# Moving sums of x, output transposes and ScalarE's bank fills in a fused attention and MLP kernel

## The chip, the cores and the metric

The kernel runs on one core of a Trainium2 chip. A core has five engines that take their instructions in order, each from its own queue, and wait for each other by semaphores: TensorE (PE in the profile; its weight loads are PEld), VectorE (DVE), ScalarE (ACT), GpSimd (POOL) and SyncE (SP), which here only issues DMAs. Times are device microseconds of one execution; the kernel before took 877.88 us in the median of three runs (873.69 to 878.38).

## The reference

Attention with a hash mask over 4 batches of 8 heads, 768 positions and 64 numbers a head, then an MLP over its 3072 tokens of 512:

```python
q_bits = (np.einsum('bhsd,dk->bhsk', q, proj) > 0).astype(np.int64)
k_bits = (np.einsum('bhsd,dk->bhsk', k, proj) > 0).astype(np.int64)
...
mask = q_bucket[:, :, :, None] == k_bucket[:, :, None, :]
scores = np.where(mask, scale * np.matmul(q, k.transpose(0, 1, 3, 2)), -1000000000.0)
attn = softmax(scores)            # with 1e-09 added to the sum
x = np.matmul(attn, v)            # brought to (3072, 512)
h = x @ w_in                      # 512 -> 2048
g = np.maximum(h, 0.0) + alpha * np.minimum(h, 0.0)
return (g @ w_out).astype(np.float32)
```

## The kernel before

`fast_path` first does the attention, in 16 pairs of heads, up to about 313 us. It stores x in DRAM (`x_s`), and rounds and stores the weights (`w_in_s`, `w_out_r`, `w_out_s`). Then comes the MLP, one batch of 768 tokens after the other, and this is where the change lies.

Both products of the MLP are done in the manner of Strassen and Winograd: a product of 2 by 2 blocks takes seven block products, on sums and differences of the blocks. The sums are made by VectorE, the products by TensorE in PSUM, and the results are put together in PSUM or by ScalarE and VectorE. `Product` (L899) is one such product in steps named 1, 2, 22, 5, 6, 3, 7, 4: each a few matmuls into one of three banks a, b, c, and a copy or a sum that reads the bank. A step's matmuls add to what stands in the bank, so ScalarE first fills ("seeds") a bank where the next sum is to start from an earlier result.

A batch b goes through 8 blocks of kind "1" (`ff1`, L966: x by w_in, with `g` made from it), n = 0 to 7, and 7 blocks of kind "2" (`ff2`, L1229: g by w_out, itself one of seven products, in the order 1, 2, 5, 6, 3, 7, 4), n = 0 to 6. The rows name the products `f_0` to `f_7` and `z_1` to `z_7`, with the bank's letter after it (`z_4a`).

For batches 1 to 3 four of the blocks "1" share two products that are done once, one level deeper: `unit(b, u, before)` (L1134), u = 0 ahead of block 0 and u = 1 ahead of block 4. A unit holds two `Inner` products, `one` and `two`, whose banks are named `na` to `nf`, and works in between the last step of the block before (`before.step(4)`) and the first steps of the block that follows. Its results are tiles named `n`. The blocks "1" after it are of the class `Rest` (L994): their step 1 seeds banks a and b with the one result, their step 5 seeds c with the other.

What each part needs from VectorE:

- `sum_x(b, n, DVE)` (L886): one subtraction of 128 by 768, making one of the four sums of x of the batch: n = 0 makes x3 from x5 and x0, n = 1 a new x5, n = 2 x4, n = 3 x6.
- `sum_inner_x(b, o)` (L1054): three subtractions (L1062 to L1064) for the nested level, `xn`; o = 0 reads x0, o = 1 reads x3.
- `sum_inner(b, u, o)` (L1046): four sums of the weights of the nested level (L1051), in batch 1 only, which are also stored by GpSimd for the later batches.
- `sum_w2(b, n, ...)` and `sum_g2(b, n, ...)` (L1211, L1221): the sums `ws` and `gs` for the next block "2". The first `sum_w2` of a block waits for the load `wl` of its part of w_out (`load_w2`, L1182).
- `turn_out()` (L1269): for each finished part of the output, two transposes by VectorE and 12 DMAs to the output, on SyncE's queue. The parts become ready at the last step of the blocks 2, 3, 7 and 4 (the entries are `m2`, `m3`, `m5`, `m4`), the last of them, `m4`, inside the unit of the next batch.

The order of the work on TensorE, VectorE, ScalarE and for most of GpSimd is the program's: `do` keeps an instruction behind all that was traced before it on its engine. DMAs are placed by the scheduler, as soon as it takes their inputs and buffers to be ready, unless they are `pinned`, which puts them behind the DMA that was traced just before on the same queue. The output DMAs of batches 0 to 2 and the loads of `load_inner` (L1021) are pinned; `load_w` (L893), which loads the `wi` weights of a block "1" three blocks ahead into one of three buffers, is not, from its fourth call on.

The loop over the blocks is at L1472. In iteration n of kind "2" it computes block n while the sums of block n + 1 are made; at its end it makes the next product and does `before.step(4)`. In blocks 6 of batches 0 to 2 it makes `sum_inner_x(b + 1, 0)`, `sum_x(b + 1, 0)`, later `sum_inner_x(b + 1, 1)`; the other three `sum_x` stand in the unit. `turn_out()` is called at the end of every iteration but the last.

Of the kernel before, what the change touches and what calls it, by code (L numbers as in the profile page):

```python
# [407 lines left out]
def fast_path(  # L408
# [14 lines left out]
    B, H, S, D = q.shape  # L423
# [20 lines left out]
    PE, DVE, ACT, POOL = nc.tensor, nc.vector, nc.scalar, nc.gpsimd  # L444
# [253 lines left out]
    def two_banks(name):  # L698
        return psum.tile([P, 2, 512], F32, name=name, tag="sc", bufs=3)
# [172 lines left out]
    def pinned(when, ins):  # L872

        if when:
            do(ins)
# [10 lines left out]
    def sum_x(b, n, engine):  # L886

        to, a, c = ((3, 5, 0), (5, 2, 5), (4, 2, 3), (6, 4, 1))[n]
        if to != 5:
            x_m[b, to] = mid.tile([P, 2, CW], F32, name=f"x{b}_{to}", tag=f"x{to}", bufs=1)  # L890
        do(engine.tensor_tensor(x_m[b, to], x_m[b, a], x_m[b, c], op=ALU.subtract))
# [102 lines left out]
    class Rest(Product):  # L994
# [5 lines left out]

        def step(self, n):
            if n == 1:
                self.seed("a", self.p1)
                self.seed("b", self.p1)
            elif n == 5:
                self.seed("c", self.p5)
            elif n == 6:
                self.times("a", 4, 4, False)
                self.keep("a", "u1")
            elif n == 7:  # L1010
                self.times("a", 5, 5, False)
                self.keep("a", "u2")
                self.finish("22", self.p5, self.sb["u2"])
            else:
                super().step(n)
# [38 lines left out]
    def sum_inner_x(b, o):  # L1054

        x = x_m[b, 3 * o]
        if o == 0:
            t = mid.tile([P, 4, HC], F32, name=f"xn{b}_0", tag="x", bufs=1)
        else:
            t = late[0].tile([P, 4, HC], F32, name=f"xn{b}_1", tag="gs5", bufs=1)  # L1060
        left, right = (x[:, :, c * HC : (c + 1) * HC] for c in range(2))
        do(DVE.tensor_tensor(t[:, :2], right, x[:, 0].rearrange("p (c w) -> p c w", c=2), op=ALU.subtract))  # L1062
        do(DVE.tensor_tensor(t[:, 2], right[:, 1], t[:, 0], op=ALU.subtract))
        do(DVE.tensor_tensor(t[:, 3], left[:, 1], t[:, 2], op=ALU.subtract))  # L1064
        n_x[b, o] = {0: left[:, 0], 1: left[:, 1], 2: right[:, 1], 3: t[:, 0], 4: t[:, 2], 5: t[:, 1], 6: t[:, 3]}
# [68 lines left out]
    def unit(b, u, before):  # L1134

        def bank(name, tag=None):
            name = f"n{name}{b}_{u}"
            return psum_bc[0].tile([P, 512], F32, name=name, tag=tag) if tag else two_banks(name)[:, 0]

        one = Inner(b, u, 0, bank("a"), bank("b", "b"), bank("c"))  # L1140
        one.step(1)
        one.step(5)
        before.step(4)
        one.step(2)
        one.step(6)
        if u:
            sum_w2(b, 0, 3, 4)
        else:
            sum_inner(b, 0, 1)
            for n in range(1, 4):  # L1150
                sum_x(b, n, DVE)
        two = Inner(b, u, 1, bank("d"), bank("e", "b"), bank("f", "c"))
        two.step(1)
        one.step(3)
        two.step(5)
        one.step(7)
        two.step(2)
        two.step(6)
        one.step(4)
        two.step(3)  # L1160
        now = ff1(b, 4 * u)
        now.step(1)
        two.step(7)
        now.step(2)
        now.step(5)
        two.step(4)
        if u:
            sum_w2(b, 0, 6, 5)
        return now

    def new_g(b, m):
# [39 lines left out]
    def sum_w2(b, n, *ms):  # L1211

        if n < 7:
            for m in ms:
                x, op, y = {
                    3: (21, ALU.add, 2), 4: (3, ALU.subtract, 0), 5: (0, ALU.subtract, 21), 6: (1, ALU.subtract, 4),
                }[m]
                w2[b, n, m] = t = late[0].tile([P, HK, H2], F32, name=f"ws{b}_{n}_{m}", tag=f"ws{m}", bufs=1 + (m < 5))
                do(DVE.tensor_tensor(t, w2[b, n, x], w2[b, n, y], op=op))  # L1219
# [49 lines left out]
    def turn_out():  # L1269
        while to_turn:  # L1270
            b, p, half, ch = to_turn.pop(0)
            o = late[0].tile([P, CW, 2], F32, name=f"o{b}_{p}", tag="o")
            for i in range(2):
                do(DVE.transpose(o[:, :, i], m2[b, p][:, i]))  # L1274

            src = o.rearrange("p (c w d) i -> p c w (d i)", c=CH, d=32)
            for a in range(DM // 128):
                for c in range(CH):
                    cols = slice(half * DM // 2 + 64 * a, half * DM // 2 + 64 * a + 64)
                    queue = nc.gpsimd if (b, p) == (B - 1, 3) and c % 2 else nc.sync  # L1280
                    pinned(b + 1 < B, queue.dma_start(  # L1281
                        out_v[b, ch * CH + c].rearrange("(w r) d -> r w d", r=32)[:, :, cols],
                        src[32 * a : 32 * a + 32, c],
                    ))
# [184 lines left out]
    blocks = [(b, what, n) for b in range(B) for what, count in (("1", NI), ("2", 7)) for n in range(count)]  # L1469


    for j, (b, what, n) in enumerate(blocks):  # L1472
        n2 = n + 1 if what == "2" else 0 if n == NI - 1 else 7
        if n2 == 0:
            sides_g(b, 0)
            if b == 0:
                sum_w2(b, 0, 3, 4)
        if not j:
            now.step(6)
        elif not (b and what == "1"):  # L1480
            now.step(2)
        if j == 0:
            now.step(3)
            now.step(7)
            now.step(2)
        now.step(22)
        if (b, what, n) == (1, "2", 1):
            largest()
        if what == "2" and n == 6 and b + 1 < B:
            sum_inner_x(b + 1, 0)  # L1490
            sum_x(b + 1, 0, DVE)
        if b and what == "1" and n == 1:
            load_inner(b, 1)
        if b and what == "1" and n in (2, 3):
            sum_inner(b, 1, n - 2)
        if 0 < n2 < 7:
            sides_g(b, n2)
            sum_w2(b, n2, 3, 4)
        if n2 < 7:
            sum_g2(b, n2, 3, 4)  # L1500
        if j:
            if not (b and what == "1"):
                now.step(5)
            now.step(6)
            now.step(3)
            if n2 or b == 0:
                sum_w2(b, n2, 6)
            if what == "2" and n == 6 and b + 1 < B:
                sum_inner(b + 1, 0, 0)
            if b and what == "1" and (n + 1) % 4:  # L1510
                after = ff1(b, n + 1)
                after.step(1)
            now.step(7)
            if n2 or b == 0:
                sum_w2(b, n2, 5)
            sum_g2(b, n2, 5)
        if (b, what, n) == (1, "2", 3):
            verdict()

        for n_out in [(), (0,), (1,), (2, 3), (4,), (5, 6), (7,)][j] if j < 7 else ():  # L1520
            sum_out(n_out)
        for n_out in [(1,), (2, 3), (4,), (5, 6), (7,)][j] if j < 5 else ():
            load_out(n_out)
        if what == "1":
            load_w(b * NI + n + 3)

            if b and n in (2, 5):
                load_w2(b, n // 4)
            if not b and n >= NI - 2:
                load_w2(b, n - NI + 2)  # L1530
        else:
            load_w2(b, n + 2)
            if b + 1 < B:
                if n == 5:
                    load_inner(b + 1, 0)
                if n == 0:
                    load_x(b + 1)
                if n == 6:
                    sum_inner_x(b + 1, 1)
        if j + 1 < len(blocks):  # L1540
            turn_out()
        else:
            turn_last(0)
        before = now
        if j + 1 < len(blocks):
            b1, what1, n1 = blocks[j + 1]
            if b1 and what1 == "1" and n1 % 4 == 0:
                now = unit(b1, n1 // 4, before)
            elif b1 and what1 == "1":
                now = after  # L1550
                now.step(2)
                now.step(5)
                before.step(4)
            else:
                now = ff1(b1, n1) if what1 == "1" else ff2(b1, n1)
                now.step(1)
                before.step(4)
        else:
            before.step(4)
        if n2 < 7:  # L1560
            sum_g2(b, n2, 6)
# [29 lines left out]
```

## Time and profile before

| | |
|---|---|
| median of three runs | 877.88 us (873.69 to 878.38) |
| the profiled execution | 873.89 us, span 872.1 us |
| TensorE busy | 855.7 us, 98% of the span |
| VectorE busy | 752.3 us, 86% |
| ScalarE busy | 415.7 us, 48% |
| GpSimd busy | 123.6 us, 14% |
| granted TensorE clock, mean | 0.997 |
| units of batches 1, 2, 3 with u = 0 start at about | 449, 589, 726 us |

The page gives the busy time of each engine; a timeline gives the instructions in order of time as "start, duration, engine, line, operation, output <- inputs, shapes, count", and in brackets how long the engine had been idle before it and who ended that. Idle time of an engine that isn't the bound costs nothing by itself. A table by stretches gives each engine's busy time in a stretch, the clock that TensorE was granted, and what the DMA engines moved. The end of a matmul is modelled, so the pauses between matmuls tell more than their durations.

### The profile page before, as it was taken

The page shows a single profiled execution, that of the slowest core. Times are in us where ns is not written, and L with a number is a line of the kernel's source. Part 1 is how long each engine was busy: PE and PEld are TensorE (multiplying, and loading weights), DVE is VectorE, ACT ScalarE, POOL GpSimd, SP SyncE. Part 2 cuts the span into 40 slices and gives each one's busy share as a digit, 9 for nine tenths or more (in the row PEclk, how much of TensorE's full clock was granted, in tenths as well). Part 3 has the DMA queues.
Part 4 walks back from the last instruction along what each step waited for, and adds up shares of the span by engine and source line. Part 5 has one row for each costly group of instructions (what it writes and reads, how often), then busy time and mean ns, then how long its engine had stood idle before and what let it go on. Part 6 is the DMA issues. An engine that isn't in the chain of part 4 may idle for free.

```text
span 872.1 us, 15105 instructions
## 1 busy us (share of the span) xinstructions
PE 855.7 (98%) x5602; PEld 591.8 (68%) x5602; DVE 752.3 (86%) x1210; ACT 415.7 (48%) x778; POOL 123.6 (14%) x265
## 2 busy tenths in 40 slices
PE   9999999999999999999989999999999999999996
PEld 4444444444444445569986759997668998577996
DVE  6999999999999977899896969896769897768986
ACT  6777888877788823321115441114452113453111
POOL 1322423332433210210000100000000000000001
PEclk9999999999999999999999999999999999999999
DMA  8855879889697536775343934342845334650242
GB/s 198 187 135 130 207 180 232 176 198 235 132 270 188 169 134 226 251 275 192 126 132 99 331 114 165 122 166 58 314 142 177 141 109 132 211 203 9 97 155 68
DMA packets 180035, 147.97 MB, mean 170 GB/s; under 512 B 126976, under 2 KB 161968, under 8 KB 176368
## 3 DMA queue, kind: packets, MB, share of 16 engines
q1 hardware_dynamic: 166688, 118.92, 46.7%
q0 software_dynamic: 10256, 26.66, 10.0%
q10 hardware_dynamic: 3008, 1.33, 0.6%
q8 instruction: 46, 0.75, 0.4%
q14 instruction: 37, 0.30, 0.1%
HBM read 115.35 MB, written 30.41 MB: 167 GB/s over the span
## 4 chain that ended last, share of the span: by engine, by line


## 5 line engine op out<-in xcount | busy, mean ns | idle before, releaser
L790 ACT ACTIVATE pt<-sc 128x768 f32<-128x768 f32 x192 | 153.9, 812 | 3.0 <-PE sc L787 2.8
L787 PE MATMUL sc<-qT,kT 64*128 64x384 f32 x768 | 155.2, 482 | 0.0
L820 PE MATMUL av<-pt,vn 128*32 128x385 f32 (+1 forms) x1536 | 127.0, 485 | 0.0
L820 PEld LDWEIGHTS av<-pt,vn 128*32 128x32 f32 x1536 | 50.4, 109 | 73.8 <-issue 68.6
L787 PEld LDWEIGHTS sc<-qT,kT 64*128 64x128 f32 x768 | 68.2, 187 | 38.1 <-issue 38.0
L983 DVE TENSOR_TENSOR g<-g,g 128x384 f32<-128x384 f32 (+1 forms) x92 | 63.5, 711 | 1.6
L787 PE MATMUL sc<-qb,kb 64*128 64x384 bf16 x384 | 63.3, 323 | 0.8 <-DVE alpha L563 0.4
L979 DVE SCALAR_TENSOR_TENSOR g<-h,alpha 128x384 f32<-128x384 f32 x63 | 37.9, 614 | 26.8 <-ACT h L972 26.8
L1281 POOL DMA_DIRECT2D out_dram<-o x4 | 2.2, 560 | 367.0 <-DVE o L1274 367.0
L1227 DVE TENSOR_TENSOR gs<-g,gs 128x768 f32<-128x768 f32 x56 | 53.3, 952 | 1.0
L1227 DVE TENSOR_TENSOR gs<-g 128x768 f32<-128x768 f32 x56 | 53.2, 951 | 0.0
L1219 DVE TENSOR_TENSOR ws<-wl 128x512 f32<-128x512 f32 x56 | 38.5, 687 | 15.9 <-DMA wl<-w_out_s 15.0
L787 PEld LDWEIGHTS <-kb 64*128 64x128 bf16 x384 | 19.4, 94 | 34.9 <-issue 11.7
L607 ACT ACTIVATE wr<-raw 128x512 int32<-128x512 uint32 x32 | 22.1, 690 | 30.7 <-DVE wsi L651 15.4
L798 DVE TENSOR_TENSOR accp<-pt,pt 128x1536 f32<-128x1536 f32 x16 | 28.1, 1756 | 7.2 <-ACT pt L790 7.2
L748 POOL DMA_DIRECT2D qb<-hr x60 | 30.0, 506 | 26.4 <-ACT hr L743 26.4
L803 DVE TENSOR_TENSOR accd<-accd,pt 128x1536 f32<-128x1536 f32 x16 | 28.1, 1758 | 1.7
L809 DVE TENSOR_TENSOR accd<-accd,accp 128x1536 f32<-128x1536 f32 x16 | 28.1, 1758 | 0.6
L806 DVE TENSOR_TENSOR accp<-accp,pt 128x1536 f32<-128x1536 f32 x16 | 28.0, 1753 | 0.0
L802 DVE TENSOR_TENSOR accd<-pt,pt 128x1536 f32<-128x1536 f32 x16 | 28.0, 1751 | 0.0
L1431 ACT ACTIVATE qT<-qT 128x768 f32<-128x768 f32 x15 | 12.7, 845 | 25.0 <-DMA kb<-hr 20.6
L1239 DVE TENSOR_TENSOR m<-m,m 128x768 f32<-128x768 f32 x24 | 22.7, 946 | 0.3
(448 smaller groups left out, 1866.2 us busy)
## 6 DMA issues: line engine op xcount, KB each, us to landing
wi<-w_in_s SPq DMA_DIRECT2D x32, 896.0 KB
wl<-w_out_s SPq DMA_DIRECT2D x16, 1024.0 KB
wl<-w_out_r SPq DMA_DIRECT2D x12, 1024.0 KB
raw<-in_moe_w_in_dram POOLq DMA_DIRECT2D x15, 512.0 KB, 4.8
raw<-in_moe_w_out_dram POOLq DMA_DIRECT2D x14, 512.0 KB, 4.8
w_in_s<-wsi SPq DMA_DIRECT2D x16, 448.0 KB
qn<-in_q_dram SPq DMA_DIRECT2D x64, 96.0 KB
vn<-in_v_dram SPq DMA_DIRECT2D x16, 384.0 KB
```

Of the source, the lines that this page charges most:

```text
L748: queue.dma_start(bits[name, pi][D * s : D * s + 2 * NB, half * CW : (half + 1) * CW], raw[c : c + 2 * NB],)
L787: do(PE.matmul(sc[:, s, :CW], what["k", pi][r, ks], what["q", pi][r, qs], start=first, stop=not first,))
L790: do(ACT.activation(pts[kc][:, g, :, :CW], sc[:, :, :CW], AF.Exp, scale=SCALE / DOWN))
L798: do(DVE.tensor_tensor(accp[pi], p(0), p(1), op=ALU.add))
L802: do(DVE.tensor_tensor(accd[pi], p(3), p(4), op=ALU.add))
L803: do(DVE.tensor_tensor(accd[pi], accd[pi], p(5), op=ALU.add))
L809: do(DVE.tensor_tensor(accd[pi], accd[pi], accp[pi], op=ALU.add))
L820: do(PE.matmul(av[pi][D * s + t : D * s + t + 32, g, :w], nat["v", pi][:, s, kc * D + t : kc * D + t + 32], pts[kc][:, g, s, :w], start=(k ...
L979: do(DVE.scalar_tensor_tensor(new_g(b, m)[:, i], h, al, h, op0=ALU.mult, op1=ALU.max))
L983: do(DVE.tensor_tensor(new_g(b, to)[:, at], g_m[b, x][:, at], g_m[b, y][:, at], op=ALU.subtract))
L1219: do(DVE.tensor_tensor(t, w2[b, n, x], w2[b, n, y], op=op))
L1227: do(DVE.tensor_tensor(t, g2[b, n, x], g2[b, n, y], op=ALU.subtract))
```

## The change

1. In `Rest.step(1)` ScalarE fills bank b ahead of bank a.
2. In `unit` with u = 0, three `sum_x` are taken out. With u = 1, `sum_w2` of the weights 3 and 4 moves from the middle of the unit to its end, where those of 6 and 5 stand.
3. `unit` calls `turn_out()` at its end. The loop's own call is left out in block 6 of kind "2", so the transposes of `m5` and of `m4` and their 24 DMAs now follow the unit with u = 0.
4. In the loop, blocks 2, 3, 4 and 5 of kind "2" each make one of the sums for the next batch, right after the read of bank b and ahead of `sum_w2`: `sum_x` 0, `sum_inner_x` 0, `sum_x` 1 and `sum_x` 2. `sum_x` 3 follows `sum_inner_x(b + 1, 1)` in block 6.

```diff
         def step(self, n):
             if n == 1:
+                self.seed("b", self.p1)
                 self.seed("a", self.p1)
-                self.seed("b", self.p1)
             elif n == 5:
                 self.seed("c", self.p5)
...
         before.step(4)
         one.step(2)
         one.step(6)
-        if u:
-            sum_w2(b, 0, 3, 4)
-        else:
+        if not u:
             sum_inner(b, 0, 1)
-            for n in range(1, 4):
-                sum_x(b, n, DVE)
         two = Inner(b, u, 1, bank("d"), bank("e", "b"), bank("f", "c"))
         two.step(1)
...
         two.step(4)
         if u:
-            sum_w2(b, 0, 6, 5)
+            sum_w2(b, 0, 3, 4, 6, 5)
+        turn_out()
         return now
...
-        if what == "2" and n == 6 and b + 1 < B:
-            sum_inner_x(b + 1, 0)
-            sum_x(b + 1, 0, DVE)
+        if what == "2" and b + 1 < B and 2 <= n < 6:
+            if n == 3:
+                sum_inner_x(b + 1, 0)
+            else:
+                sum_x(b + 1, {2: 0, 4: 1, 5: 2}[n], DVE)
...
                 if n == 6:
                     sum_inner_x(b + 1, 1)
-        if j + 1 < len(blocks):
+                    sum_x(b + 1, 3, DVE)
+        if j + 1 == len(blocks):
+            turn_last(0)
+        elif what == "1" or n < 6:
             turn_out()
-        else:
-            turn_last(0)
         before = now
```

## The prediction

> **What bounds the kernel now.** I read the page first, then TensorE's instructions in order of time, then what ends TensorE's pauses.
>
> ```profile
> span 872.1 us, 15105 instructions
> ...
> PE 855.7 (98%) x5602; PEld 591.8 (68%) x5602; DVE 752.3 (86%) x1210; ACT 415.7 (48%) x778; POOL 123.6 (14%) x265
> ```
>
> TensorE (PE) is the bound. In order of time its records touch each other nearly everywhere; only the pauses can be won, and nearly all of those after the attention stand in the nested units. The number in brackets is the pause before the row, and who ended it:
>
> ```profile
> 452.43 0.92 PE L1084 MATMUL nc<-xn,wn 128*128 128x192 f32 x4 [2.30 <-DVE wn L1051]
> ...
> 499.72 1.56 PE L921 MATMUL f_4b<-x,wi 128*128 128x384 f32 x4 [0.57 <-ACT f_4b L999]
> ...
> 594.66 0.92 PE L1084 MATMUL nd<-x,wq 128*128 128x192 f32 x4 [1.62 <-DVE m L1246]
> ...
> 731.13 0.92 PE L1084 MATMUL nd<-x,wq 128*128 128x192 f32 x4 [1.48 <-DVE m L1246]
> ```
>
> The 0.57 recurs at 636.58 and 773.05. With 0.18 at 486.56 these are 7.3 us: all there is. The first costs more than its 2.30. In 3.41 us stretches (columns: length, PE, PEld, DVE, ACT, POOL busy with counts, clock, DMA share, GB/s):
>
> ```profile
> 450.21:453.62 3.41, 1.19 (x7) 1.20 (x8) 3.27 (x9) 0.62 (x2) 0.95 (x2) 1.00 0.21 51
> 453.62:457.03 3.41, 3.41 (x13) 3.41 (x12) 2.65 (x8) 0.28 (x1) 1.20 (x3) 0.50 0.42 163
> 457.03:460.44 3.41, 3.41 (x23) 3.41 (x22) 3.38 (x7) 1.60 (x4) 2.14 (x4) 1.00 0.47 134
> ```
>
> After a stretch with TensorE busy for 1.19 of 3.41 us the next ran at half clock. From `nc` to `nd` it took 5.03 us (452.43 to 457.46); undisturbed it is 3.25 (589.63 to 592.88), so 1.78 more.
>
> VectorE (DVE) before the 1.62 us pause:
>
> ```profile
> 592.07 0.55 DVE L1062 TENSOR_TENSOR xn<-x 128x384 f32<-128x384 f32 x1
> ...
> 593.33 1.04 DVE L1274 STREAM_TRANSPOSE o<-m 128x384 f32<-128x384 f32 x2
> 594.29 0.32 DVE L1246 TENSOR_TENSOR m<-m,z_4a 128x192 f32<-128x192 f32 x1
> ```
>
> The read of `z_4a` that frees `nd`'s bank comes last on a VectorE that has had no pause since 569.72; `nd` could have started at 593.04. VectorE's pauses lie earlier, at the w_out loads:
>
> ```profile
> 552.33 0.69 DVE L1219 TENSOR_TENSOR ws<-wl 128x512 f32<-128x512 f32 x1 [2.87 <-DMA wl<-w_out_s]
> ...
> 569.72 0.69 DVE L1219 TENSOR_TENSOR ws<-wl 128x512 f32<-128x512 f32 x1 [0.28 <-DMA wl<-w_out_s]
> ...
> 714.98 0.69 DVE L1219 TENSOR_TENSOR ws<-wl 128x512 f32<-128x512 f32 x1 [0.19 <-DMA wl<-w_out_r]
> ```
>
> SyncE's queue after a unit:
>
> ```profile
> 586.81 13.11 SPq L1281 DMA_DIRECT2D out_dram<-o  x24
> 609.53 0.34 SPq L897 DMA_DIRECT2D wi<-w_in_s  x1
> 609.98 6.66 SPq L1281 DMA_DIRECT2D out_dram<-o  x12
> 616.68 0.43 SPq L1025 DMA_DIRECT2D wn<-w_in_s  x1
> ```
>
> One output transpose issues 12 DMAs at 0.546 us each. The `wi` between is block 3's weights, issued when block 0 is done with the buffer.
>
> **What the Trainium skill says.** "TensorE: Matmul & The Clock Gate", Part 1: TensorE falls to half clock after an idle window of about 3.4 us, and the windows run freely. The length agrees (3.41 us); here a window busy for 1.19 us sufficed, so the measurement decides; one busy for 2.32 us (593.56 to 596.98) did not. Same page, "Architectural detail": VectorE and ScalarE are strict queues. The trace agrees: at 552.33 everything stands behind one load. "DMA: Bandwidth & Descriptors", "Anatomy of one DMA": a DMA's semaphore wait is on the issuing sequencer, before dispatch; the SP rows agree, one issue after another, so a late load is late for all behind it.
>
> **The change part by part** (times of the profile before).
>
> *Sums of x.* Per batch, `sum_x` is 0.87 us from start to start (588.69 to 590.81 holds one and a `sum_inner_x`) and `sum_inner_x` 1.25. Five sums leave the wait of TensorE: 1.25 + 0.87 before the first reads of `z_4`, and three `sum_x` (2.80) behind `two`'s start. They go to blocks 2, 3, 4, 5, ahead of the `ws` wait (0.87, 1.25, 0.87, 0.87), and one (0.87) stands in block 6 where the transposes (0.97) stood. The pauses there are 1.21, 1.34, 1.10, 0.22 in batch 0 and 1.29, 1.36, 1.07, 0.19 in batch 2, so VectorE is late only after block 5, by 0.65 and 0.68. In batch 1 they are 2.87, 0, 0.28, 0: late by 1.25, 1.8, 2.65. The inputs `x` were issued at 494 to 525, 25 us ahead; without that cover each sum would wait.
>
> - *Batch 0 to 1.* The first `wn` sum starts at 451.95 - 2.12 + 0.65 = 450.48, `nc` 0.47 later at 450.95: pause 0.83 in place of 2.30, too short for the half clock. Next late is `nd`, behind the second `sum_inner_x` and a `sum_x`: `z_4a` read at 454.35 to 454.66, `nd` at 454.70 in place of 457.46. Gain 2.76.
> - *Batch 2 to 3.* The read comes at 730.76 - 2.22 + 0.68 = 729.22, done 729.54; TensorE is ready at 729.65. Gain 1.48, and 0.10 for a prefetched weight load (`nd` takes 0.75, its likes 0.65): 1.58.
> - *Batch 1 to 2.* The read comes at 594.29 - 2.22 + 2.65 = 594.72, `nd` at 595.1: 0.4 lost. On the way `z_7c` and `z_4c` wait 0.4 and 0.55 for their bank, included there. If the load at 552.33 comes as promptly as its twins, VectorE is 1.45 late and 0.8 is won. I take the middle, 0.2.
>
> *Sums of w_out in the second unit* go behind it. `n L1125` then starts when the four `L983` end, 1.3 us earlier, and ScalarE's seeds no longer wait (0.41). With b seeded first, it is full at 635.6; TensorE's `nd` ends at 636.01. The pause of 0.57 and 0.10 of the slower start go, three times: 2.0. Four sums (2.6 us) then follow the unit in place of two; the `g` behind had 0.86 of wait, so it slips 0.4, covered by the 1.14 before the next `f_4u`.
>
> *Seeds swapped.* For `f_0b` the seed is ready 0.41 earlier; the pause is only 0.06, and 0.11 of slow start: 0.5 for three. Bank a is needed 2 us later (602.88), so nothing waits for it; in the other Rest blocks the later seed ends 0.8 early (605.65 against 606.43).
>
> *Output transposes behind the unit.* Four in a row (2.0 us) after `n L1129`, at 601.92 to 603.9, where VectorE waits 2.10 for `h`: free, and up to 2.0 a batch without that wait. GpSimd's queue is not passed. But they issue 24 DMAs in a row from 602.98: 24 x 0.546 = 13.1, until 616.1. The order in the queue is the scheduler's: before, block 3's `wi` preceded the last 12, because the pinned outputs stand behind what was traced before them. Now the outputs are traced first and are ready 6.5 us sooner, so I take `wi` to stand behind all 24. Issued at 616.1 instead of 609.53, it lands 4.0 later (packets of the old one ran to 613.5) at 620.1. `f_3b` wants it at 619.65 - 0.18 = 619.47: a pause of 0.65 and the lost prefetch, 0.8 each. Behind SP's `wi` stands the second half's `wn`; its bytes queue behind 3 us of `wi`. In batches 2 and 3 they land by 624, wanted at 625.8. In batch 1 VectorE sums them at 483.98 and would get them at 485.0; behind it wait `f_2u`, ScalarE's `f_3c` seed, TensorE: 1.2 there in all. Cost 0.8 + 0.8 + 1.2 = 2.8; bounds 0 (`wi` slips between the outputs) and, with outputs at the 0.705 us (16.93 for 24) seen at 445.97, 13.
>
> Sum: 2.76 + 0.2 + 1.58 + 2.0 + 0.5 - 2.8 = 4.2 us gained. The profiled execution took 873.89 (span 872.1 and 1.8 around): 869.7 after. The runs shown are 873.69, 877.88, 878.38, median 4 above the profile. The page doesn't say why. One reading: the pauses at 594.66 and 731.13 lie 136.47 us apart, 40 stretches of 3.41, so both fall whole into a window or neither does; two more half-clock stretches (1.7 to 2 each) would be those 4 us, and would go with the pauses. I take 870.
>
> **The rivals.**
>
> *`wi` in time.* The scheduler places it among the outputs: no 2.8, 866.9. For it: it chose well before. Against: outputs ready first.
>
> *The gain is eaten.* VectorE is late in batch 1 throughout, `wi` lands a us later, and the 4 us of the median have another cause: a gain of 2 to 3, so 871 to 875, within 0.5%. For it: 86% busy VectorE, no pause after 569.72.
>
> *SyncE becomes the bound: slower.* One mechanism: outputs ahead of `wi`. At 0.705 us each, `wi` goes at 619.9, lands 623.9; `f_3b` pauses 4.4, three times 13.2 against 7.0 won: 880. It decides when the pause passes 2.35, that is at 0.617 us an output. For it: the 24 at 445.97; against: those ran beside GpSimd's stores, which end before 465.
>
> **How the numbers follow.** `wi` behind the outputs, 0.45; in time, 0.17; eaten, 0.25; slower, 0.13. The first two are faster by over 0.5% (4.4 us, about what a measurement of this kernel tells from no change) of the median, 0.62. Range 865.8 to 876.5: from `wi` in time with 1 us more, to the eaten case with the high state of the runs.
>
> **What would show it.** Right: no 2.30 before `nc`, no half clock near 454, no 0.57 before `f_4b`, `nd` pauses gone in batch 3 and left in batch 2; L1281 x24 with `wi` behind it, and a new pause before `f_3b` three times, released by a DMA. Wrong: `f_3b` without a pause (faster), or pauses over 2 us there or before `z_7c`, `z_4c` (slower).

## The result, and the profile after

The changed kernel takes 867.4 us in the median (866.14 to 868.89, 5 runs). The kernel before, on the same chip, takes 875.72 (873.69 to 878.38, 5 runs). The ratio is 0.990, with a 95% interval of 0.9875 to 0.9926. The forecast was 870.0, within 865.8 to 876.5, so the change won about one and a half times what was forecast against the profiled execution's own time: 873.89 became 867.4, and the span fell by 6.5 us, not by 4.2. The medians differ by 8.3 us. The profiled execution of before was one of its faster runs, that of the changed kernel its median one, so what follows accounts for 6.5 of these 8.3.

The page of the changed kernel:

```profile
span 865.6 us, 15105 instructions
PE 853.1 (99%) x5602; PEld 590.5 (68%) x5602; DVE 751.6 (87%) x1210; ACT 415.7 (48%) x778; POOL 123.8 (14%) x265
```

The work is the same: as many instructions, VectorE as busy as before. TensorE is busy for 2.6 us less, which is above all the half-clock stretch that is gone (1.7 us), and its pauses are shorter. The timeline of TensorE after (start, duration, engine, line, operation, tiles; in brackets the pause before it and who ended it):

```profile
451.22 0.92 PE L1084 MATMUL nc<-xn,wn 128*128 128x192 f32 x4 [0.80 <-DVE wn L1051]
...
455.00 0.92 PE L1084 MATMUL nd<-x,wq 128*128 128x192 f32 x4 [0.27 <-DVE m L1243]
...
590.71 0.92 PE L1084 MATMUL nd<-x,wq 128*128 128x192 f32 x4 [1.00 <-DVE m L1243]
...
724.94 0.92 PE L1084 MATMUL nd<-x,wq 128*128 128x192 f32 x4 [0.32 <-DVE m L1243]
...
750.69 1.53 PE L921 MATMUL f_3b<-x,wi 128*128 128x384 f32 x4 [0.93 <-DMA wi<-w_in_s]
```

(The read of `z_4a`, L1246 before, is L1243 here.) The 2.30 before `nc` is 0.80, the 1.62 and 1.48 before `nd` are 1.00 and 0.32, and the three pauses before `f_4b` are gone. New are a pause of 0.27 before `nd` in batch 1 and one of 0.93 before `f_3b` in batch 3, ended by a DMA. (One of 0.37 before `z_2c` in batch 0 comes and goes between profiles of the same kernel, as shown below.) In the table by stretches of the changed kernel (length, PE, PEld, DVE, ACT, POOL busy, clock, DMA share, GB/s) the place around `nc` keeps full clock:

```profile
449.19:452.60 3.41, 2.61 (x16) 2.31 (x15) 3.17 (x11) 1.18 (x3) 1.14 (x3) 1.00 0.32 76
452.60:456.01 3.41, 3.14 (x20) 2.85 (x19) 3.31 (x8) 0.63 (x3) 1.02 (x2) 1.00 0.47 172
```

Setting the start of each TensorE row against the same row of before gives the time won by place:

| place | forecast, us won | measured |
|---|---|---|
| `nc`, `nd`, half clock in batch 0 to 1 | 2.76 | 2.65 (2.75 up to the start of `nd`, 0.10 lost at its first matmul) |
| batch 1 to 2 | 0.2 | 0.42 (0.13, then -0.33 at `z_4c`, then 0.62 at `nd`) |
| `nd` in batch 2 to 3 | 1.58 | 1.07 |
| `f_4b`, three times | 2.0 | 2.52 (0.84 each) |
| `f_0b`, three times | 0.5 | 1.00 (0.33 each) |
| `f_3b` and what follows it, late weights | -2.8 | -1.16 (batch 3 only; in batch 1 0.16, given back at `f_3c`) |
| elsewhere | 0 | 0.25 in the attention, -0.54 at `z_2c` in batch 0, 0.30 at the end |
| sum | 4.2 | 6.5 |

SyncE's queue after the change:

```profile
463.20 11.28 SPq L1278 DMA_DIRECT2D out_dram<-o  x24
474.57 0.38 SPq L897 DMA_DIRECT2D wi<-w_in_s  x1
475.00 0.43 SPq L1025 DMA_DIRECT2D wn<-w_in_s  x1
...
598.91 11.40 SPq L1278 DMA_DIRECT2D out_dram<-o  x24
610.41 0.38 SPq L897 DMA_DIRECT2D wi<-w_in_s  x1
...
733.14 12.67 SPq L1278 DMA_DIRECT2D out_dram<-o  x24
745.90 0.38 SPq L897 DMA_DIRECT2D wi<-w_in_s  x1
```

Block 3's `wi` does stand behind all 24 outputs, in all three batches, with the second half's `wn` right behind it, as forecast. But in batches 1 and 2 the 24 outputs take 11.3 to 11.4 us, so 0.47 us each, not 0.546. In batch 3 they take 12.67: one issue there is 1.86 ahead of the next, and the others are 0.47 apart as well. Why that one is slow is open. The forecast's 0.546 was 13.11 / 24, from one row of the kernel before. Asked for in two stretches, that row of the kernel before comes apart:

```profile
586.81 6.94 SPq L1281 DMA_DIRECT2D out_dram<-o  x12
```

and

```profile
594.39 5.53 SPq L1281 DMA_DIRECT2D out_dram<-o  x12
```

The second dozen takes 0.46 each. The first takes 0.58: five of its issues are 0.46 to 0.51 apart, and then a few are 0.6 to 1.4 apart. Between the dozens stands a gap, while the second transpose was not done. All this went into the mean. The 0.705 us of the forecast's upper bound (24 outputs at 445.97) was read in the same way: a pause of 4.06 us stands between its dozens.

### The profile page after: what moved, and what is told of

Its sections match the earlier page's. It is cut to its first block, busy times and chain, and to the rows that moved or that the text cites. A ratio compares the mean times of both kernels' runs of the same rounds, so it can differ in the third digit from the quotient of the medians.

```text
span 865.6 us, 15105 instructions
## 1 busy us (share of the span) xinstructions
PE 853.1 (99%) x5602; PEld 590.5 (68%) x5602; DVE 751.6 (87%) x1210; ACT 415.7 (48%) x778; POOL 123.8 (14%) x265
## 4 chain that ended last, share of the span: by engine, by line
```

## Experiments

Ratios are to the kernel before, run beside it on the same chip; the interval behind each is a 95% interval.

**The kernel before once more.**

> The kernel before, once more, for a second profile at another phase of the clock windows. Theory (half clock): the runs of before differ by whole stretches at half clock, about 1.7 us each, tripped by the pauses at 452, 594 and 731 us; another profile shows the same pauses to 0.1 us, but half clock at other places or more of it, and its time follows the number of such stretches (873.9 with one, about 877.5 with three). Rival: the pauses and the half clock are the same in every profile and the 4 us between runs lie elsewhere, in the attention. Ratio 1.000 either way.

Measured: 875.87, ratio 1.0007 (0.9992 to 1.0021). The kernel before ran 67 times on this chip: median 875.56, from 872.51 to 880.6, in one hump. There are not two groups 4 us apart, as the forecast's reading of the runs' spread (two more half-clock stretches in the slower runs) would have it. The expectation that the pauses come back to 0.1 us failed too: here they are 2.52 before `nc` and 1.48 and 1.85 before `nd`, against 2.30, 1.62 and 1.48, with one half-clock stretch as before. So a difference of up to 0.4 us in one pause between two profiles means nothing by itself. What differs as well is small waits for loads: VectorE waited for w_out's loads in batch 0 for 1.72, 1.08, 1.29 and 0.35 us here, against 1.21, 1.34, 1.10 and 0.22 in the profile shown ahead, and TensorE's pause at `z_2c`, which the change doesn't touch, is 0.78 here and nothing there.

**ScalarE's seeds alone.**

```diff
             if n == 1:
+                self.seed("b", self.p1)
                 self.seed("a", self.p1)
-                self.seed("b", self.p1)
```

> The swapped seeds alone. Theory (the parts add): the pause of 0.57 before f_4b falls to about 0.16, f_0b starts 0.2 to 0.3 earlier, three times each: 2.0 us less, ratio 0.998. Nothing else moves: 2.30 before nc, 1.62 and 1.48 before nd stay. Rival: the second seed is late in the Rest blocks, so that what is won at f_4b is given back at f_4a: ratio 1.000.

Measured: 873.0, ratio 0.9978 (0.9965 to 0.9991). TensorE's timeline of this kernel:

```profile
497.82 1.56 PE L921 MATMUL f_4b<-x,wi 128*128 128x384 f32 x4 [0.17 <-ACT f_4b L999]
...
593.04 0.92 PE L1084 MATMUL nd<-x,wq 128*128 128x192 f32 x4 [1.85 <-DVE m L1246]
```

The swap takes the pause before `f_4b` from 0.57 to 0.17 (0.16 in the other batches) and the one before `f_0b` to nothing. That is 1.4 us of pauses in all. By the starts of TensorE's rows `f_4b` wins 0.40 and `f_0b` 0.33 a time, 2.2 us together; the ratio says 1.9 us, with an interval from 0.8 to 3.1. The pause before `nd`, which this edit does not touch, is 1.85 in this profile (1.62 before), and the half-clock stretch follows it, at 594, while the 2.46 before `nc` brings none.

**w_out's sums behind the second unit alone.**

```diff
-        if u:
-            sum_w2(b, 0, 3, 4)
-        else:
+        if not u:
...
         if u:
-            sum_w2(b, 0, 6, 5)
+            sum_w2(b, 0, 3, 4, 6, 5)
```

> The sums of w_out behind the second unit alone. Theory: n L1125 comes 1.3 us earlier, ScalarE's seeds 0.4, and with bank a still filled first bank b is full 0.1 after TensorE wants it: the pause before f_4b falls from 0.57 to 0.1, three times, 1.5 us less, ratio 0.998. Rival: ScalarE's second seed is what the 0.57 waits for, and it comes no earlier: pause and ratio stay.

Measured: 872.6, ratio 0.9977 (0.9967 to 0.9987). The pause before `f_4b` is 0.06 in all three batches. By the rows' starts that wins 0.50 a time: less than the 0.84 of both edits together, because the pause of 0.06 that is left has the same 0.27 us of lost time behind it as the one of 0.57 (see the part on `f_4b` below). The seeds alone win 0.40, so the two nearly add up. In the changed kernel ScalarE no longer waits for `n L1125`, and fills `f_4b` first:

```profile
630.84 0.49 ACT L999 COPY f_4b<-n 128x384 f32<-128x384 f32 x1
631.26 0.49 ACT L999 COPY f_4a<-n 128x384 f32<-128x384 f32 x1
```

**The sums of x alone.**

```diff
             sum_inner(b, 0, 1)
-            for n in range(1, 4):
-                sum_x(b, n, DVE)
...
-        if what == "2" and n == 6 and b + 1 < B:
-            sum_inner_x(b + 1, 0)
-            sum_x(b + 1, 0, DVE)
+        if what == "2" and b + 1 < B and 2 <= n < 6:
+            if n == 3:
+                sum_inner_x(b + 1, 0)
+            else:
+                sum_x(b + 1, {2: 0, 4: 1, 5: 2}[n], DVE)
...
                     sum_inner_x(b + 1, 1)
+                    sum_x(b + 1, 3, DVE)
```

> The sums of x alone, with transposes, seeds and sums of w_out as before. Theory (the parts add): nc's pause falls from 2.30 to 0.8 with no half clock behind it, 1.8 us less up to nd; but in block 6 a sum_x now stands beside the transposes, so z_4a is read about 1 us later than in the changed kernel: pauses before nd of 1.2, 2.0 and 1.3 us. In all 1 to 2 us faster, ratio 0.998 to 0.999, and slower than that where the 2.0 us pause trips the half clock. Rival: the sums carry the whole gain by themselves, ratio 0.993 or less.

Measured: 873.57, ratio 0.998 (0.9968 to 0.9992). The pause before `nc` falls to 0.74, and the half clock near 454 is gone. But the pauses before `nd` are 1.19, 1.92 and 1.57 in the three batches: no better than before in batches 2 and 3, and new in batch 1. VectorE's timeline tells why, here in batch 2 to 3, first of the kernel before:

```profile
724.88 0.35 DVE L1246 TENSOR_TENSOR m<-m,z_4b 128x192 f32<-128x192 f32 x1
...
730.76 0.32 DVE L1246 TENSOR_TENSOR m<-m,z_4a 128x192 f32<-128x192 f32 x1
```

and then with the sums moved alone:

```profile
726.22 0.35 DVE L1244 TENSOR_TENSOR m<-m,z_4b 128x192 f32<-128x192 f32 x1
...
729.01 0.95 DVE L891 TENSOR_TENSOR x<-x,x 128x768 f32<-128x768 f32 x1
729.88 1.03 DVE L1272 STREAM_TRANSPOSE o<-m 128x384 f32<-128x384 f32 x2
730.83 0.32 DVE L1244 TENSOR_TENSOR m<-m,z_4a 128x192 f32<-128x192 f32 x1
```

From the read of `z_4b` to that of `z_4a` it needs 4.61 us instead of 5.88, since `sum_x` 3 and the transposes still stand in between. And it comes to `z_4b` 1.34 later, though TensorE's rows stand within 0.1 us of those of before: the sums filled VectorE's pauses, and a load that it still waits for in block 4 came 0.75 later (706.66 instead of 705.91). The wait was moved, not removed. (The forecast for this place counts on the transposes' going as well.)

**The transposes behind the unit alone.**

```diff
         if u:
             sum_w2(b, 0, 6, 5)
+        turn_out()
         return now
...
-        if j + 1 < len(blocks):
-            turn_out()
-        else:
+        if j + 1 == len(blocks):
             turn_last(0)
+        elif what == "1" or n < 6:
+            turn_out()
```

> The output transposes behind the unit alone. Theory (the parts add): z_4a is read 0.97 earlier, so the pauses before nd fall from 1.62 and 1.48 to about 0.6 and 0.5 (2.0 us less); 2.30 before nc and its half clock stay; SyncE issues 24 outputs in a row at 0.46 each ahead of block 3's weights, and f_3b pauses for 0 to 1.1 us: 1 to 2 us faster, ratio 0.998 to 0.999. Rival (outputs in the way): the weights of block 3 come late in all three batches by 0.8 us or more, ratio 1.000.

Measured: 873.24, ratio 0.9976 (0.9966 to 0.9987). TensorE's timeline:

```profile
453.99 1.65 PE L1084 MATMUL nc<-xn,wn 128*128 128x192 f32 x4 [2.58 <-DVE wn L1051]
...
595.00 0.92 PE L1084 MATMUL nd<-x,wq 128*128 128x192 f32 x4 [0.69 <-DVE m L1247]
```

The pause before `nd` in batch 2 falls by 0.93 (from 1.62) and the one in batch 3 to 0.44, by 1.04: the two transposes (0.97). The pause before `nc` stays, and with it the half clock, here at 453.51 (`nc` itself takes 1.65). `f_3b` pauses in batch 3 alone, by 0.62; the 24 outputs ahead of its `wi` take 12.46 us there, with one step of 1.69 between two issues.

**The changed kernel without the moved transposes.**

```diff
             sum_w2(b, 0, 3, 4, 6, 5)
-        turn_out()
         return now
...
-        if j + 1 == len(blocks):
+        if j + 1 < len(blocks):
+            turn_out()
+        else:
             turn_last(0)
-        elif what == "1" or n < 6:
-            turn_out()
```

> The changed kernel with the output transposes back where they were. Theory (the parts add, but sums and transposes share block 6): z_4a is read about 1 us later in each transition, so nd pauses for 1.2, 2.0 and 1.3, and f_3b's pause is gone: 2 to 2.5 us slower than the changed kernel, ratio to before 0.993. Where the 2.0 trips the half clock, 1.7 more. Rival (outputs in the way): without the 24 outputs ahead of block 3's weights it is as fast as the changed kernel, ratio 0.990.

Measured: 870.5, ratio 0.9948 (0.9928 to 0.9968); the expectation had 0.993. Beside it the **changed kernel once more**:

> The changed kernel once more, beside the next three on one chip. Theory (the parts add): ratio 0.990 as before; the pauses before nc (0.8) and nd (0.3, 1.0, 0.3) return to 0.2 us, no half clock after them, and f_3b pauses for up to 1 us in one or more batches, by how late the outputs leave SyncE. Rival: the profile of the changed kernel was a lucky one, and a second shows f_3b paused in all three batches, or the half clock; ratio 0.993 or more.

Measured: 866.76, ratio 0.9908 (0.9891 to 0.9926). The second profile has pauses of 0.60 before `nc` and of 0.27, 0.98 and 0 before `nd`, and before `f_3b` it has one in batch 3 alone:

```profile
748.70 1.53 PE L921 MATMUL f_3b<-x,wi 128*128 128x384 f32 x4 [0.19 <-DMA wi<-w_in_s]
```

That is 0.19 where the first profile had 0.93; the 24 outputs ahead took 12.03 us, with one step of 1.22 between two issues where the first profile had one of 1.86. So the price of the outputs in batch 3 differs from run to run.

Inside the whole the transposes are worth 0.40% by these ratios, against 0.24% alone. The intervals overlap, so the times don't show that it is more. Alone, the move takes 2.0 us off the pauses before `nd`, and in the whole, where `sum_x` 3 has come into block 6, 2.3 and a half-clock stretch. Without it `nd` pauses again by 1.19, 1.92 and 0.74, and this 1.92 brought the clock down, as the table by stretches of this kernel shows:

```profile
590.37:593.78 3.41, 1.49 (x10) 1.19 (x9) 3.16 (x7) 0.48 (x1) 0.00 (x0) 1.00 0.22 50
593.78:597.20 3.42, 3.42 (x12) 3.42 (x11) 0.56 (x1) 0.84 (x2) 0.00 (x0) 0.50 0.28 67
```

In this kernel, where `wi` goes ahead of the last 12 outputs, `f_3b` has no pause.

**Only the outputs of `m4` behind block 3's weights.** The transposes stay behind the unit; the last 12 DMAs are kept back until the next `turn_out()`, behind `wi`.

```diff
-        turn_out()
+        turn_out(hold=not u)
...
+    held = []
+    def turn_out(hold=False):
+        while held:
+            send(*held.pop(0))
...
+            if hold and not to_turn:
+                held.append((o, b, p, half, ch))
+            else:
+                send(o, b, p, half, ch)
```

> The changed kernel, but the last 12 of the 24 outputs behind the unit, those of m4, are issued only behind block 3's weights wi; nothing is left out. My theory: what wi loses by standing behind 24 outputs instead of 12 is 12 issues of 0.46 to 0.47 us, 5.6 us (wi was issued at 474.57, 610.41 and 745.90). So wi goes 5 to 6 us earlier in each batch, f_3b has no pause in batch 3 (0.93 in the changed kernel) and no slow start in batches 1 and 3, TensorE gains 0.16 and 1.16 us there, 1.3 us in all, and no other pause is new: span 863.5 to 864.5, ratio to the kernel before 0.989 to 0.991. Rival 1: the prediction's price for it, 2.8 us, was right and the trace of the changed kernel hides part of it: span 862 to 863, ratio about 0.987. Rival 2: f_3b waits for something else as well (packets of other queues, not wi's place), and the pause before f_3b in batch 3 stays at 0.5 us or more.

Measured: 867.7, ratio 0.9904 (0.9887 to 0.9922). The profiled execution had a span of 868.5, longer than any theory said. TensorE's timeline:

```profile
453.35 0.92 PE L1084 MATMUL nc<-xn,wn 128*128 128x192 f32 x4 [1.60 <-DVE wn L1051]
...
753.20 1.45 PE L921 MATMUL f_3b<-x,wi 128*128 128x384 f32 x4
```

and SyncE's queue:

```profile
743.08 0.34 SPq L897 DMA_DIRECT2D wi<-w_in_s  x1
743.52 6.52 SPq L1274 DMA_DIRECT2D out_dram<-o  x12
```

`f_3b` in batch 3 has no pause, and against the changed kernel's first profile TensorE wins 1.16 us there. So the place of `wi` behind the last 12 outputs is what `f_3b` waited for, and its price was 1.16 us in that profile, not 2.8; against the second profile it is 0.43. In batch 1 the 0.16 won is lost again before `f_3c`. The span is longer than the changed kernel's by 2.9 us. Of these 2.1 are lost ahead of the first unit, where the edit begins: in batch 0 VectorE waits 1.32 for a load of w_out at 441.70 (the changed kernel's profile has no such wait), and `nc` pauses 1.60 instead of 0.80. Another 1.4 are lost behind it, in batch 1 before `z_6a`, `z_7c` and `z_4c` (more of that below), and 0.5 at the end. The medians (867.7, and 867.4 and 866.76 for the changed kernel) can't show a difference of 1 us.

**A version that takes up what was left.** With the outputs held as above, `sum_x` 3 moves behind the read of `z_4a`, and the weight sums of the first nested product start right after step 22 of block 6.

```diff
         if not u:
             sum_inner(b, 0, 1)
+            sum_x(b, 3, DVE)
...
+        if what == "2" and n == 6 and b + 1 < B:
+            sum_inner(b + 1, 0, 0)
...
-            if what == "2" and n == 6 and b + 1 < B:
-                sum_inner(b + 1, 0, 0)
...
                     sum_inner_x(b + 1, 1)
-                    sum_x(b + 1, 3, DVE)
```

> The changed kernel with three more moves: the last sum of x behind the read of z_4a, the first nested sums of w_in (batch 1) ahead of the reads of z_4's other quarters, and the 12 output DMAs of m4 behind the load of block 3's weights. Theory: nc's 0.8 goes, nd pauses for 0, 0.1 and 0, f_3b for 0: 2.5 to 3.5 us less than the changed kernel, ratio to before 0.986 to 0.987. Rival: VectorE, late since block 3, is then waited for at the next place (nf or f_0), and no more than 1 us is won.

Measured: 865.86 (863.1 to 868.39), ratio 0.9895 (0.9873 to 0.9918). The 2.5 to 3.5 us of the theory did not come; what was won is the rival's 1 us, though at other places than it named. The pauses before `nc` and `f_3b` are gone, and those before `nd` are 0.40, 0.13 and 0. In their place TensorE's timeline has two small ones in batch 1:

```profile
572.02 1.57 PE L921 MATMUL z_7c<-gs,ws 128*128 128x192 f32 x8 [0.24 <-DVE m L1246]
...
581.68 1.57 PE L921 MATMUL z_4c<-gs,ws 128*128 128x192 f32 x8 [0.29 <-DVE m L1246]
```

They are the pauses that the forecast put at 0.4 and 0.55: VectorE late behind a load in batch 1. They go with when that load comes. In the four kernels with the moved sums in which `wi` goes ahead of the last 12 outputs (sums alone, without the moved transposes, and the two with outputs held) VectorE waits for it 1.92 to 2.53 us, and both pauses are there, 0.23 to 0.29 each. In both profiles of the changed kernel it waits 1.01 and 0.79, and `z_7c` has none. Why the load is earlier there isn't settled: the order in the queue alone doesn't do it, since with the transposes alone, where `wi` is behind all outputs too, the wait is 2.73, which is 1.86 with the 0.87 of a sum taken off. So holding the outputs back may give in batch 1 what it wins in batch 3. About 1 us of pauses is won over the changed kernel; its median is 0.9 below the 866.76 of the changed kernel that ran beside it, but the intervals overlap, so it isn't shown to be faster.

## Why the prediction was right, and where its sum was wrong

- *Batch 0 to 1* was right in size (2.65 against 2.76) and in mechanism: the pause before `nc` fell below 1 us, the half clock went, and `nd` stands at 455.00 (454.70 forecast). The sums alone shorten this pause (0.74); with each other part alone it stays at 2.3 to 2.6. That the half clock went is no luck of one profile: the mean granted clock is 0.9962 in the 97 runs of the kernel before that ran beside the experiments, and 0.9981 in the 11 of the changed kernel. A stretch of 3.41 us at half clock takes 0.0020 off the mean of 872 us, so a run has about one such stretch less.
- *Batch 2 to 3* (1.58 forecast, 1.07 measured): VectorE's reads of `z_4b` and `z_4a` are 3.66 apart (720.88 to 724.54) instead of 5.88, which is the 2.22 of the working. What was low was the lateness ahead of it: against TensorE's rows VectorE comes to `z_4b` 1.04 later than before, not 0.68, and a pause of 0.32 stayed. (The second profile has none.) The forecast moved the loads of w_out not at all; the one that VectorE still waits for in block 4 came 0.5 later.
- *Batch 1 to 2* (0.2 forecast, 0.42 measured) lay in its bounds of -0.4 to 0.8. The 0.2 was the middle between a load that stays late and one that comes promptly, so that it is near is luck. The late load at 552.33 came more promptly: VectorE's timeline after shows a wait of 1.01 behind the first sum, where 2.87 stood; 0.87 of the difference is the sum, 0.99 the load. (By the forecast's own terms VectorE's lateness is 1.25 + 0.87 - 0.28 + 0.87 = 2.71, not 2.65.)

```profile
547.95 0.69 DVE L1216 TENSOR_TENSOR ws<-wl 128x512 f32<-128x512 f32 x1 [1.01 <-DMA wl<-w_out_s]
...
590.31 0.35 DVE L1243 TENSOR_TENSOR m<-m,z_4a 128x192 f32<-128x192 f32 x1
```

- *`f_4b` and `f_0b`* gave 3.5 instead of 2.5. The pauses were right (0.57 and 0.06); what goes beyond them is 0.27 a time in both, where the forecast had 0.10 and 0.11 for the slower start of matmuls after a pause. That slower start is right too: the first matmul takes 0.59 where its likes take 0.49. The forecast put the other 0.16 at nothing. A pause is counted from the modelled end of the matmul before it, and in an unbroken stream the next one starts before that end, as in the changed kernel:

```profile
495.65 0.81 PE L1084 MATMUL nd<-xn,wp 128*128 128x192 f32 x4
496.30 1.45 PE L921 MATMUL f_4b<-x,wi 128*128 128x384 f32 x4
```

The `nd` row ends at 496.46 and `f_4b` starts at 496.30, 0.16 earlier. So a pause in these rows is 0.16 us longer than it reads, and a row without one can still be late (`f_3b` in batch 1 by 0.08).

- *The output DMAs* are the step that failed in size: "24 x 0.546 = 13.1". An output takes 0.47 us, but for a few slower ones, above all one in batch 3. The order in the queue was right. Against the start of `nd` in batch 2, `wi` leaves 4.8 us later than before (19.70 against 14.87), where the forecast had 6.6 at an unmoved `nd`; the old transfer's last packet ended at 614.1, not at 613.5 as the forecast reads it, so 5.4 before `f_3b` wanted it (619.47), and in these traces `f_3b` starts 0.45 after the last packet at the soonest (750.22 to 750.69 in batch 3). That leaves a margin of 4.9, just more than the slip, so nothing shows in batch 2. In batch 3 the 24 took 12.67 (733.14 to 745.81), near the forecast's 13.1, and `f_3b` waited 0.93, near its 0.65. This was not for the forecast's reason: at 0.47 throughout, `wi` would have left 1.4 us earlier, and as `f_3b` started 4.8 after it, that is an estimate of no pause at all. The 1.2 us for batch 1, where late `wn` was to hold up VectorE, did not come: 1.16 in all instead of 2.8 (0.43 in the second profile). This is 1.64 of the 2.3 us that the sum was short of; `f_4b` and `f_0b` are 1.0, and the other places take 0.4 back. Of the signs that were to show the forecast right, the new pause before `f_3b` thus came once, not three times.
- *The rivals.* 867.4 is the number of the rival "`wi` in time" (866.9), but not by its mechanism: `wi` was not in time in the queue, only cheaper. "SyncE becomes the bound" decides from 0.617 us an output; the 24 took 0.47 each in two batches and 0.53 in the third. "The gain is eaten" fell with batch 1.
- *The half clock as a cause of the runs' spread* was a conjecture, and it holds for a small part at most. Of the 67 runs of the kernel before, the 30 with a mean granted clock of 0.997 took 875.1 us on average and the 6 with 0.993, about two half-clock stretches more, 876.2: 1.1 us, where the forecast had 4. The forecast's step from 869.7 to 870 leaned on it. Against the 877.88 shown ahead, 870 is 0.9% less, as was measured; but 4 of these 7.9 us rested on this conjecture, so the agreement in per cent is in part luck. Why two of the first three runs lay high is open; the kernel before varies by 8 us from run to run, and its profiles differ in waits for loads.

The parts alone sum to 0.22 + 0.20 + 0.24 + 0.23 = 0.89%, and the whole is 0.9 to 1.0%. Each part has an interval of about 0.1% either way and the whole one of 0.2 to 0.25%, so they agree, but an overlap between parts of a tenth of a per cent would not show. By TensorE's rows the seeds and w_out's sums win 3.7 us one by one and 3.5 together. That the sums of x and the transposes help each other is seen in the traces alone, by the 0.3 us of pauses and the half-clock stretch above.

## What to carry to other kernels

Moving an engine's work ahead of a wait can leave the engine as late as before: look at the whole stretch from its last real pause to the read that TensorE waits for, as the sums of x alone showed. Before you divide the length of a merged row by its count, ask for the row in two halves: a gap inside becomes a price that nobody pays. Before you price one pause from one profile, take a second profile of the same kernel: here the pause before `f_3b` was 0.93 in one and 0.19 in the other. Where a DMA slips behind others in a queue, its cost is the slip minus the margin with which it used to land, and the margin is read from the landing of the old one and from how soon after it its reader starts.

## What was not expected of the hardware

A pause of TensorE brings the half clock or not, depending on where it falls. The clock records change only at multiples of 3.413 us (in the kernel before 447.15 us at full clock ahead of the half-clock stretch, which is 131 of them). Cutting each trace into these stretches, ahead of the last matmul the half clock followed six, with TensorE busy for 0.94, 1.19, 1.31, 1.49, 1.56 and 1.56 us. It followed none with 1.80 or more. The one exception, with 1.49 and full clock after it, is shown below. The sums alone paused for 1.92 us like the version without the moved transposes, but kept full clock, for there the pause fell across a boundary:

```profile
590.42:593.84 3.42, 2.28 (x15) 1.99 (x13) 3.25 (x9) 0.72 (x2) 0.00 (x0) 1.00 0.42 101
593.84:597.25 3.41, 2.63 (x16) 2.63 (x17) 1.75 (x5) 0.83 (x2) 0.00 (x0) 1.00 0.26 61
```

"TensorE: Matmul & The Clock Gate", Part 1 of the Trainium skill, speaks of an idle window; here a stretch that was busy for 46% sufficed (1.56 of 3.41). The exception is in the kernel with w_out's sums moved alone, where 1.49 us did not bring it and 1.56 us later did:

```profile
450.22:453.63 3.41, 1.49 (x9) 1.49 (x10) 3.27 (x10) 0.61 (x2) 1.25 (x3) 1.00 0.21 58
...
726.70:730.11 3.41, 1.56 (x10) 1.27 (x9) 3.34 (x9) 0.48 (x1) 0.00 (x0) 1.00 0.16 37
730.11:733.52 3.41, 3.41 (x13) 3.41 (x12) 2.74 (x4) 0.94 (x2) 0.00 (x0) 0.50 0.28 68
```

What else decides is open. No trace had two half-clock stretches between 380 us and the last matmul.
